# Attention products in tiles of 64 rows by 32 columns, with two accumulators for the weighing, on one Trainium2 core

## The chip, the cores and the metric

The kernel runs on one core of one Trainium2 chip. A core has TensorE (PE in the profile, with its weight loads as PEld), VectorE (DVE), ScalarE (ACT), GpSimd (POOL) and SyncE (SP, which here only issues DMAs). The metric is the device time of one execution in microseconds (us); the kernel before takes 2609.37 us, the median of three runs.

## The reference

One transformer block on 2048 tokens of width 576: attention of 32 heads (18 wide each), then a gated feed-forward part 4608 wide.

```python
qkv = (x @ wqkv).reshape(B, S, 3, H, Dh).transpose(2, 0, 3, 1, 4)
scores = jnp.einsum("bhqd,bhkd->bhqk", q, k) * Dh ** -0.5
p = softmax(scores);  o = jnp.einsum("bhqk,bhkd->bhqd", p, v)
h = x + A(layernorm(x))          # A: the attention above, then @ wo
out = h + B(layernorm(h))        # B: (gelu(z @ w_gate) * (z @ w_up)) @ w_down
```

## The kernel before, in words

Matrices that need more than 16 bits are held as a high and a low half-precision part, and a product is made of three matmuls or of stacked rows. A head is 18 wide; its Q and K are stacked as high and low parts in 54 rows (plus 2 rows that carry the row's maximum), and two heads share a tile, one from row 0 and one from row 64 (`half`).

The attention runs in 32 blocks n = 0 to 31: eight groups g of four heads, and for each group four query blocks qc of 512 queries. A block has 16 key tiles kt of 128 keys, and a key tile is one *step*. The string `STEPS[kt % 2]` sets the order of the work in a step by letters:

- `s`: `score` (L659 to L667). One matmul of 128 keys by 512 queries for one head, and ACT's exponential of it into SBUF (L667). Four in a step.
- `m`: `max_bank` (L607 to L625). The maxima for the *next* block: one matmul of 128 queries by 512 keys (L615), then a reduction over the keys. Of eight such units DVE alone reduces six (L625); for one pair ACT takes a Relu of a difference (L619, "over") and DVE finishes the pair with a fused add and maximum (L623, "both"). Four in a step.
- `w`: half a `weigh` (L669 to L677). Four matmuls (one for each head, 128 keys by 32 columns of V, in fp32) add the weighted values of the step before to an accumulator, for 256 of the 512 queries. V has a column of ones, so the accumulator also holds the softmax's divisor.
- `f`: two pieces of other matmul work (`fill`) and one piece of work for POOL (`side`).

Scores and maxima take turns in a ring of seven PSUM banks (`m_ring`), and the weighing's accumulator is the eighth (`singles[3]`, bank in the profile). At the end of a block `out_block` (L682) copies the accumulator to SBUF (L688, on DVE; for the last two blocks on ACT), fetches the divisors by DMA, takes reciprocals on POOL (L698 and on; on DVE in the last group), sends them back as rows by DMA, multiplies and splits on POOL (L711, L712, L713), and sends the result to the tensor XT (X in the profile) by DMAs on SP (L726 to L730). It is a generator: its parts are taken at key tiles 3 and 5 of the next block, in the last blocks (29 to 31) at 3 and 6.

In the last group two more things run beside the attention. `fill` is `wo_block` (from key tile 12 of blocks 29 to 31): the output projection of the query block that was just finished, as runs of 14 matmuls (L300) which read X; an `f` takes two runs. `side` is `split_early` on POOL (L1039 and on): it scales and splits the feed-forward weights (L1055, L1056, L1058, L1059) and then issues the next weights' DMAs on POOL's queue (L977, L979). The order of instructions on each engine is the order in which the program issues them.

## Time and profile before

| | |
|---|---|
| runs | 2608.49, 2609.37, 2609.64 us |
| profiled execution, span from first to last instruction | 2604.1 us, 53642 instructions |
| PE | 2579.3 us busy, 99% |
| DVE | 2010.0 us, 77% |
| ACT | 1661.3 us, 64% |
| POOL | 818.9 us, 31% |
| granted TensorE clock | 1.000 |
| plain attention block (1 to 28) | 35.84 us |
| blocks 29, 30, 31 | about 47.9, 49.1, 38.0 us |

The page gives no time of the profiled execution other than its span; the runs' median is 5.3 us longer. In a row of a timeline the columns are start, duration, engine, line, operation, output and inputs, shapes, count, and in brackets the idle time before it with what ended it. `nat`, `A`, `W`, `WK` and `X` are SBUF tensors of which parts are used for many things; `bank` and `quad` are PSUM banks.

### The profile page before, as it was taken

The numbers are of one execution on the slowest core, as the hardware profiler recorded it, in microseconds if no ns is written. First come the engines' busy times: TensorE is split into PE (matmuls) and PEld (weight loads), VectorE is DVE, ScalarE is ACT, GpSimd is POOL, SyncE is SP. The second block draws the span as 40 slices with busy tenths as digits, with TensorE's granted clock in tenths as the row PEclk, the third lists the DMA queues.
The fourth block names the chain that finished last, engine by engine and source line by source line (L and its number), as shares of the span: only waits on it lengthen the run. The fifth ranks groups of instructions, "written<-read, shape, count | busy, mean of one in ns | idle before, by whom it ended". The sixth has DMA issues, their size and how long they took to land.

```text
span 2604.1 us, 53642 instructions
## 1 busy us (share of the span) xinstructions
PE 2579.3 (99%) x20765; PEld 1198.2 (46%) x20765; DVE 2010.0 (77%) x3886; ACT 1661.3 (64%) x3124; POOL 818.9 (31%) x1146
## 2 busy tenths in 40 slices
PE   8999999999999999999999999999999999999999
PEld 4543333333333333333335555555555555555555
DVE  8479999999999999999867675757565656565653
ACT  6229999999999999999774543424243433333332
POOL 4302532322223232324585432323232323222221
PEclk9999999999999999999999999999999999999999
DMA  8621010101001010101135410101010101010110
GB/s 227 154 77 45 17 47 17 44 19 39 20 23 41 16 43 16 47 16 32 38 64 116 83 34 30 34 30 34 30 34 30 34 30 34 30 34 30 34 56 37
DMA packets 170193, 118.23 MB, mean 45 GB/s; under 512 B 88664, under 2 KB 147564, under 8 KB 169938
## 3 DMA queue, kind: packets, MB, share of 16 engines
q1 hardware_dynamic: 161198, 98.47, 14.2%
q0 software_dynamic: 8608, 16.33, 2.6%
q8 instruction: 162, 2.65, 0.4%
q14 instruction: 93, 0.76, 0.1%
q10 hardware_dynamic: 132, 0.01, 0.0%
HBM read 80.05 MB, written 15.01 MB: 37 GB/s over the span
## 4 chain that ended last, share of the span: by engine, by line
PE 92%; DVE 4%; POOL 1%; DMA 1%; issue 1%; ACT 1%; SPq 0%; POOLq 0%; ACTq 0%
PE bank L673 19%; PE bank L1125 15%; PE more L1125 15%; PE bank L300 11%; PE more L300 8%; PE quad L615 7%; PE bank L615 6%; PE quad L300 4%; PE quad L665 4%; DVE mx L625 3%; PE bank L665 3%; DVE nat L688 1%; DMA A<-qk_hi 0%; POOL A L1055 0%; ACT A L155 0%
## 5 line engine op out<-in xcount | busy, mean ns | idle before, releaser
L667 ACT ACTIVATE WK<-quad 128x512 f32<-128x512 f32 x1170 | 656.2, 621 | 23.4 <-PE quad L665 21.0
L673 PE MATMUL bank<-WK,V 128*32 128x256 f32 x8192 | 606.6, 388 | 2.7 <-DVE nat L688 0.6
L625 DVE TENSOR_REDUCE mx<-quad 128x1 f32<-128x512 f32 x836 | 553.8, 684 | 9.0 <-PE quad L665 1.5
L667 ACT ACTIVATE WK<-bank 128x512 f32<-128x512 f32 x878 | 504.9, 622 | 11.1 <-PE bank L665 9.3
L625 DVE TENSOR_REDUCE mx<-bank 128x1 f32<-128x512 f32 x716 | 477.1, 684 | 33.5 <-PE bank L615 26.4
L300 PEld LDWEIGHTS <-WK 128*128 128x128 f16 x3456 | 338.2, 98 | 88.3
L1125 PEld LDWEIGHTS <-W 128*128 128x128 f16 x2394 | 234.3, 98 | 278.3
L673 PEld LDWEIGHTS bank<-WK,V 128*32 128x32 f32 x8192 | 190.0, 108 | 268.2 <-issue 201.3
L300 PE MATMUL more<-W,WK 128*128 128x288 f16 x1728 | 235.2, 286 | 0.0
L300 PE MATMUL bank<-W,WK 128*128 128x288 f16 x1728 | 235.2, 286 | 0.0
L698 POOL TENSOR_TENSOR rp<-rc,minus_one 128x4 f32<-128x4 f32 x112 | 111.2, 1012 | 383.9 <-DMA rc<-nat 383.9
L1125 PE MATMUL bank<-X,W 128*128 128x512 f16 x792 | 223.8, 379 | 0.0
L1125 PE MATMUL bank<-V,W 128*128 128x512 f16 x720 | 202.4, 379 | 0.0
L993 POOL TENSOR_TENSOR A<-A 128x384 f32<-128x384 f32 x136 | 138.1, 1036 | 200.2 <-DMA A<-in_B_w_up_dram 83.7
L615 PE MATMUL quad<-W 54*128 54x512 f16 x514 | 191.0, 382 | 0.2 <-DVE mx L625 0.2
L615 PEld LDWEIGHTS <-W 54*128 54x128 f16 x1024 | 74.5, 94 | 241.3 <-issue 226.8
L1139 POOL TENSOR_TENSOR WK<-tmp,WK 128x512 f16<-128x512 f32 x73 | 88.5, 1212 | 305.8 <-ACT WK L1136 305.6
L615 PEld LDWEIGHTS <-A 54*128 54x128 f16 x1024 | 71.1, 94 | 231.0 <-issue 216.7
L1143 ACT COPY tmp<-more 128x512 f32<-128x512 f32 x36 | 20.9, 582 | 238.3 <-PE more L1125 203.4
L665 PE MATMUL quad<-A 56*128 56x512 f16 x584 | 172.1, 380 | 0.3
L615 PE MATMUL quad<-A 54*128 54x512 f16 x462 | 171.6, 382 | 0.1
L665 PE MATMUL quad<-W 56*128 56x512 f16 x586 | 167.5, 380 | 0.1
(348 smaller groups left out, 4122.3 us busy)
## 6 DMA issues: line engine op xcount, KB each, us to landing
A<-in_B_w_down_dram SPq DMA_DIRECT2D x8, 1152.0 KB
nat<-rc SPq DMA_DIRECT2D x32, 256.0 KB
A<-in_B_w_gate_dram SPq DMA_DIRECT2D x64, 128.0 KB
A<-in_B_w_up_dram SPq DMA_DIRECT2D x64, 128.0 KB
qk_hi<-tmp SPq DMA_DIRECT2D x36, 128.0 KB
qk_lo<-tmp SPq DMA_DIRECT2D x36, 128.0 KB
out_dram<-nat SPq DMA_DIRECT2D x16, 288.0 KB
X<-nat SPq DMA_DIRECT2D x100, 36.0 KB
```

The lines of the kernel that those rows point to most:

```text
L300: nc.tensor.matmul(dst, a, b, start=(i == 0), stop=(i == len(pairs) - 1))
L615: nc.tensor.matmul(pm[:, :TB], Q[r, q0 : q0 + P], keys, start=True, stop=True)
L625: nc.vector.tensor_reduce(dst, pm[:, :TB], axis=AX.X, op=ALU.max)
L665: nc.tensor.matmul(pS[:, :TB], K[r, kt * P : (kt + 1) * P], Q[r, qc * TB : (qc + 1) * TB], start=True, stop=True)
L667: nc.scalar.activation(pes[(2 * kt + hh // 2) % NPE][:, hh % 2], pS[:, :TB], AF.Exp, scale=ex_reg)
L673: nc.tensor.matmul(acc[32 * hh : 32 * hh + 32, qs], Vg[n // NB][:, kt * G4 + hh * VC : kt * G4 + hh * VC + 32], pes[(2 * kt + hh // 2) % N ...
L688: (nc.scalar.copy if n >= NS - 2 else nc.vector.tensor_copy)(oT, acc[:, :TB])
L698: nc.gpsimd.tensor_tensor(rc[:, c : c + 4], den[:, c : c + 4], minus_one.to_broadcast([P, 4]), op=ALU.pow)
L993: op(W8[:, d], W8[:, a], W8[:, b])
L1125: nc.tensor.matmul(bank, w, x_, start=start and i == 0, stop=i == len(mm) - 1, skip_group_check=not start)
L1139: nc.gpsimd.tensor_sub(hl[:, 2 * i + j], v, hh[:, 2 * i + j])
L1143: nc.scalar.copy(xg, g[0])
```

## The change

Every matmul of the attention is issued in tiles of 64 rows by 32 columns. A score or a maximum becomes four loads and four matmuls (L618, L670), each for 32 of its 128 output rows, on the row half of its head. Half a weighing becomes eight matmuls (L679): four columns by two row halves, and the two halves of the keys go to two accumulators, `singles[3]` and `quads[3]`. The ring has six banks instead of seven. `out_block` copies the first accumulator on ACT (L693) and the second on DVE, into `oT2`, and POOL adds the two (L696); for the last two blocks DVE adds the second one from PSUM. The steps have a new order, in which the halves of the weighing wait in a queue (one is taken in an even step, three in an odd one) and `f` comes last. The parts of `out_block` are taken one key tile later. The maxima come in an order in which two neighbours of one row half follow two of the other. Before the first block 93 maxima are taken ahead, 96 before.

```diff
--- before.py
+++ after.py
@@ -1,5 +1,6 @@
 import math
 from contextlib import ExitStack
+from collections import deque
 from itertools import chain, islice
 
 import concourse.bass as bass
@@ -573,6 +574,7 @@
     steps = [view(nat1, 12288 + 4 * TB * i, (HB, TB), F16) for i in range(2)]
     rows_of = ring([view(nat1, 18432 + 4 * TB * i, (TB,)) for i in range(2)])
     LOWEST = -3.0e38
+    CT = 32
     excess = []
     DQ = 4
     DI = TB // DQ
@@ -612,7 +614,9 @@
         r = half(h % 2, R1)
         pm = next(m_ring)
         keys = steps[g % 2][r, kc // 2] if kind == "over" else K[r, kc * TB : (kc + 1) * TB]
-        nc.tensor.matmul(pm[:, :TB], Q[r, q0 : q0 + P], keys, start=True, stop=True)
+        for c in range(0, P, CT):
+            nc.tensor.matmul(pm[c : c + CT, :TB], Q[r, q0 + c : q0 + c + CT], keys,
+                             start=True, stop=True)
         dst = mx[:, t, h, kc : kc + 1]
         if kind == "over":
             row = next(rows_of)
@@ -662,30 +666,36 @@
         pS = next(m_ring)
         Q, K = sets[g % 2][hh // 2]
         r = half(hh % 2, R1 + 2)
-        nc.tensor.matmul(pS[:, :TB], K[r, kt * P : (kt + 1) * P],
-                         Q[r, qc * TB : (qc + 1) * TB], start=True, stop=True)
+        for c in range(0, P, CT):
+            nc.tensor.matmul(pS[c : c + CT, :TB], K[r, kt * P + c : kt * P + c + CT],
+                             Q[r, qc * TB : (qc + 1) * TB], start=True, stop=True)
         nc.scalar.activation(pes[(2 * kt + hh // 2) % NPE][:, hh % 2], pS[:, :TB], AF.Exp, scale=ex_reg)
 
-    def weigh(n, kt, acc):
-        for q in range(2):
-            qs = slice(q * TB // 2, (q + 1) * TB // 2)
+    def weigh(n, kt, accs, q):
+        qs = slice(q * TB // 2, (q + 1) * TB // 2)
+        for i, acc in enumerate(accs):
+            ks = slice(64 * i, 64 * i + 64)
             for hh in range(4):
-                nc.tensor.matmul(acc[32 * hh : 32 * hh + 32, qs],
-                                 Vg[n // NB][:, kt * G4 + hh * VC : kt * G4 + hh * VC + 32],
-                                 pes[(2 * kt + hh // 2) % NPE][:, hh % 2, qs],
+                nc.tensor.matmul(acc[CT * hh : CT * hh + CT, qs],
+                                 Vg[n // NB][ks, kt * G4 + hh * VC : kt * G4 + hh * VC + CT],
+                                 pes[(2 * kt + hh // 2) % NPE][ks, hh % 2, qs],
                                  start=(kt == 0 and q == 0), stop=(kt == NT - 1 and q == 1))
-            yield
 
     minus_one = const.tile([P, 1], F32, name="minus_one")
     nc.gpsimd.memset(minus_one, -1.0)
 
-    def out_block(n, acc):
-
-
+    oT2 = view(nat1, 16384, (TB,))
+
+    def out_block(n, accs):
 
         g, qc = divmod(n, NB)
         oT = oTs[n % 2]
-        (nc.scalar.copy if n >= NS - 2 else nc.vector.tensor_copy)(oT, acc[:, :TB])
+        nc.scalar.copy(oT, accs[0][:, :TB])
+        if n < NS - 2:
+            nc.vector.tensor_copy(oT2, accs[1][:, :TB])
+            nc.gpsimd.tensor_add(oT, oT, oT2)
+        else:
+            nc.vector.tensor_add(oT, accs[1][:, :TB], oT)
         R = 4 * TB // P
         rc = small.tile([P, R], F32, tag="rc", name="rc")
         (nc.scalar if n == NS - 1 else nc.sync).dma_start(rc, oT.rearrange("(h c) q -> h c q", c=32)[:, DH].rearrange(
@@ -744,8 +754,8 @@
                 nc.gpsimd.memset(mx[:, :, 0, 1::2], LOWEST)
             for u in range(0, UPS, 2):
                 t, k = divmod(u, NB)
-                for unit in (("one", t, k, 1), (over, t, k + 1, 0), ("one", t, k + 1, 1), ("one", t, k, 2),
-                             ("one", t, k, 3), (both, t, k, 0), ("one", t, k + 1, 2), ("one", t, k + 1, 3)):
+                for unit in (("one", t, k, 1), ("one", t, k + 1, 1), ("one", t, k, 2), (over, t, k + 1, 0),
+                             ("one", t, k, 3), ("one", t, k + 1, 3), (both, t, k, 0), ("one", t, k + 1, 2)):
                     max_bank(n, mx, *unit)
                     yield
             max_finish(n, mx)
@@ -1246,40 +1256,40 @@
     side = iter(())
     take(fill, 18)
     for i in range(5 * AHEAD // 4):
-        take(mxs, 3 + (i % 5 == 4))
+        take(mxs, 1 if i == 5 * AHEAD // 4 - 1 else 3 + (i % 5 == 4))
         if i == AHEAD // 4:
             raw_loads()
         if i >= AHEAD // 3:
             take(sums)
         take(fill, 2 + (i % 5 == 2))
     run(sums)
-    m_ring = ring(singles[:3] + quads)
-    STEPS = ("ssmsmmfwmsw", "mssmssmfwwm")
-    OUT_AT = STEPS[0].rindex("w")
-    prev = None
+    m_ring = ring(singles[:3] + quads[:3])
+    accs = (singles[3], quads[3])
+    STEPS = ("smsmwsmsf", "wsmssmmwsmmwf")
+    halves = deque([None, None])
     for n in range(NS):
         g, qc = divmod(n, NB)
-        acc = singles[3]
         late = n > NS - NB
         for kt in range(NT):
             heads = iter(range(4))
-            halves = weigh(*prev) if prev is not None else iter(())
-            for step_no, step in enumerate(STEPS[kt % 2]):
+            for step in STEPS[kt % 2]:
                 if step == "s":
                     score(n, kt, next(heads))
                 elif step == "m":
                     take(mxs)
                 elif step == "w":
-                    take(halves)
-                    if kt == 0 and step_no == OUT_AT and prev is not None:
-                        ob = out_block(prev[0], prev[2])
-                        next(ob)
+                    half_ = halves.popleft()
+                    if half_ is not None:
+                        weigh(*half_)
+                        if half_[1] == NT - 1 and half_[3] == 1:
+                            ob = out_block(half_[0], accs)
+                            next(ob)
                 else:
                     if n < NS - 1 or kt < 11:
                         take(fill, 2)
                     take(side)
-            prev = (n, kt, acc)
-            if n and kt in ((1 if n == NS - 1 else 3, 6) if late else (3, 5)):
+            halves += [(n, kt, accs, q) for q in range(2)]
+            if n and kt in ((2 if n == NS - 1 else 4, 7) if late else (4, 6)):
                 take(ob)
             if late and kt == 11:
                 run(fill)
@@ -1308,8 +1318,9 @@
                              pause(2), until_ready(second))
     in_order.enter_context(tc.manual_schedule(engines={EngineType.SP}))
     run(side)
-    run(weigh(*prev))
-    ob = out_block(prev[0], prev[2])
+    for half_ in halves:
+        weigh(*half_)
+    ob = out_block(NS - 1, accs)
     next(ob)
     for _ in fill:
         take(rows, 2)
```

What stands on PE's queue in the middle of a block, before: a maximum, half a weighing, a maximum, a score, the other half (`quad` and `bank` are ring banks, bank_69 is the accumulator, A, W and WK hold Q, K and the exponentials).

```order
L615 MATMUL quad_76<-A 128x512
L673 MATMUL bank_69<-WK,V 32x256 x4
L615 LDWEIGHTS A
L615 MATMUL bank_66<-A 128x512
L665 LDWEIGHTS A
L665 MATMUL bank_67<-A 128x512
L673 MATMUL bank_69<-WK,V 32x256 x4
```

And now, at a like place, a maximum, a score and half a weighing; each of the first two stands there four times, once for each 32 of its output rows.

```order
L618 LDWEIGHTS W
L618 MATMUL quad_73<-W 32x512
...
L670 LDWEIGHTS A
L670 MATMUL quad_74<-A 32x512
...
L679 MATMUL bank_69<-WK,V 32x256 x4
L679 MATMUL quad_76<-WK,V 32x256 x4
```

The output of one matmul is 32 rows instead of 128, and the weighing has a second accumulator, quad_76, which was a bank of the ring.

ACT's queue at the start of a block, now: the copy of the first accumulator (bank_69) between exponentials. Before, no copy stood there except in the last two blocks.

```order
L672 ACTIVATE WK<-bank_66 128x512
L672 ACTIVATE WK<-bank_68 128x512
L693 COPY nat<-bank_69 128x512
L672 ACTIVATE WK<-quad_73 128x512
L672 ACTIVATE WK<-quad_75 128x512
```

POOL's queue in block 30, before: the end of a piece of weight splitting, the three instructions that make the rows of X, then the first two of eight weight DMAs (an L1055 and L1056 of the next piece come behind the eighth).

```order
L1058 TENSOR_TENSOR WK<-A,W 128x256
L1059 TENSOR_TENSOR W<-A,W 32x128
L711 TENSOR_TENSOR nat<-nat 128x512
L712 CAST nat<-nat 128x512
L713 TENSOR_TENSOR nat<-nat 128x512
L977 DMA A<-in_B_w_gate_dram 128x2x128
L979 DMA A<-in_B_w_gate_dram 96x1x128
```

And now the place from the eighth DMA on:

```order
L989 DMA A<-in_B_w_gate_dram 96x1x128
L1065 TENSOR_SCALAR A<-A,p_s_m_30894 128x768
L1066 CAST W<-A 128x768
L721 TENSOR_TENSOR nat<-nat 128x512
L722 CAST nat<-nat 128x512
L723 TENSOR_TENSOR nat<-nat 128x512
L1068 TENSOR_TENSOR WK<-A,W 128x512
```

The eight DMAs and the first two instructions of the next piece have passed ahead of the three that make X (L711 to L713 are L721 to L723 now). In block 29 the eight DMAs stood ahead already; there the new addition L696 stands at the head of the splitting, and one L1065 and L1066 more stand ahead of L721.

## The prediction, as put on record before the changed kernel ran

> **What bounds the kernel now.** I read the span first, then busy time by stretch, then the queues of each engine inside one stretch.

> ```profile
> core 0: 2604.1 us, clock 1.000
> ```

> ```profile
> 563.30:599.14 35.84, 35.76 (x390) 11.54 (x388) 35.31 (x67) 35.72 (x74) 8.39 (x14) 1.00 0.05 15
> 1244.50:1292.40 47.90, 44.97 (x449) 18.50 (x446) 40.68 (x85) 36.26 (x74) 32.42 (x45) 1.00 0.15 39
> 1292.40:1341.50 49.10, 48.00 (x473) 21.36 (x471) 27.21 (x59) 34.77 (x70) 34.66 (x57) 1.00 0.18 50
> ```

> The second fence is the view of busy time by stretch: after start, end and length come PE, PEld, DVE, ACT and POOL, each with its count, then the clock. The first row is one plain attention block of 35.84 us (16 key tiles), of which there are 28, blocks 1 to 28. Here PE, ACT and DVE all look full, so shares don't decide. The other two rows are blocks 29 and 30, which also carry the output projection of an earlier block; they are 12 and 13 us longer, and only PE is near full. So there are two stages with two limits. In the plain stage the question is which engine is full by its own rate. Groups of instructions over ten plain blocks, and ACT's and DVE's queues inside one:

> ```profile
> L667 ACT ACTIVATE WK<-quad 128x512 f32<-128x512 f32 x367 | 206.2, 622 | 0.6
> L667 ACT ACTIVATE WK<-bank 128x512 f32<-128x512 f32 x274 | 157.9, 621 | 0.5
> ```

> ```profile
> 703.62 0.65 ACT L667 ACTIVATE WK<-bank 128x512 f32<-128x512 f32 x1
> 704.10 0.67 ACT L619 ACTIVATE nat<-bank 128x512 f32<-128x512 f32 x1
> 704.58 0.68 ACT L667 ACTIVATE WK<-quad 128x512 f32<-128x512 f32 x1
> ```

> ```profile
> 703.82 1.28 DVE L625 TENSOR_REDUCE mx<-quad 128x1 f32<-128x512 f32 x2
> ```

> ACT ends at 704.27, 704.77 and 705.26: 0.49 us each, though a record is 0.65 long, since neighbours overlap. By the code ACT has 64 exponentials and 8 Relus in a block: 72 × 0.49 = 35.3 of 35.84, and the idle column is 1.1 us in ten blocks. ACT is full. A pair of DVE reductions takes 1.28, one alone 0.68, so one costs 0.60; 48 reductions, 8 double ones (L623) and one copy (L688) are 57 × 0.60 = 34.2 us, 1.6 below the block. Now PE over one step and the loads beside it:

> ```profile
> 701.19 1.07 PE L673 MATMUL bank<-WK,V 128*32 128x256 f32 x16
> 702.19 0.39 PE L615 MATMUL quad<-W 54*128 54x512 f16 x1
> 702.20 0.60 PE L665 MATMUL quad<-W 56*128 56x512 f16 x2
> 702.42 0.38 PE L665 MATMUL bank<-W 56*128 56x512 f16 x1
> 702.64 0.38 PE L615 MATMUL bank<-W 54*128 54x512 f16 x1
> 702.86 0.37 PE L615 MATMUL bank<-nat,W 54*128 54x512 f16 x1
> 702.86 0.39 PE L615 MATMUL quad<-W 54*128 54x512 f16 x1
> 703.18 0.64 PE L673 MATMUL bank<-WK,V 128*32 128x256 f32 x8
> 703.75 0.39 PE L615 MATMUL quad<-W 54*128 54x512 f16 x1
> ```

> ```profile
> 700.22 0.11 PEld L665 LDWEIGHTS <-W 56*128 56x128 f16 x2
> 700.23 0.10 PEld L615 LDWEIGHTS <-W 54*128 54x128 f16 x1
> ...
> 703.18 0.16 PEld L673 LDWEIGHTS bank<-WK,V 128*32 128x32 f32 x8 [0.23 <-issue]
> ```

> Score and maximum matmuls start 0.22 apart, two at a time where they sit on different row halves (702.86 twice). Sixteen weighing matmuls last 1.07 and eight 0.64, so eight cost 0.43, two slots of 0.22. The first weighing after a score starts 0.32 behind the last score (0.10 over a slot), and eight weighings last 0.57 until the next score (0.14 over two slots): a change between the two tile shapes costs about 0.12. Two steps (4.42 us) hold 16 scores and maxima in pairs, 8 slots, four half weighings, 8 slots, and six changes: 16 × 0.22 + 6 × 0.12 = 4.24. PE is close behind ACT, but ACT, not PE, sets the 35.84.

> **The change part by part.** *Tiles, plain stage.* A score is now four column tiles side by side on one row half, still one slot; a half weighing is eight tiles side by side, four columns by two halves, still 2 × 0.22. The six changes go: PE falls from 4.24 to 16 × 0.22 = 3.5 us per two steps. As ACT needs 9 × 0.49 = 4.41, this buys at most ACT's remaining idle time, 35.84 − 35.3 = 0.54 per block.

> *The second accumulator.* DVE keeps its copy (now of the second accumulator), POOL gets an addition, and ACT gets the copy of the first, in the queue of the full engine: 0.49 per block. With PE's slack taking all of the old idle time, a block is 73 × 0.49 = 35.75 (−0.09); with all of it staying, 36.33 (+0.49). The idle time sat mostly around DVE's copy and the end of a block's maxima, where PE now has 0.9 us per two steps to catch up, but six banks in the ring instead of seven hold less work for ACT (6 × 0.49/2 on average, since about half go to DVE). I take −0.02 per block, near the low end: 28 × −0.02 = **−0.5**, bounds −2.5 and +14.

> *Records.* Two steps issue 256 loads and matmuls instead of 96, so 17 ns for each in 4.42 us. The densest row above is eight loads within 0.16 us, each about 0.10 long: (0.16 − 0.10)/7 = 9 ns apart. The longest possible reading is 32 records in the 1.00 us of the sixteen weighings, 31 ns, but that stretch is explained by four slots of array time. I take 9 ns, so nothing; the other end is a rival below.

> *Loads.* A score's load of 0.10 is now four loads on 32 columns each. At 700.22 to 700.23 three loads of both halves run together while the matmuls of both halves are just beginning, so a load waits for no slot, and the sum has nothing for it. [...]

> *Late blocks, tiles.* Ten times in blocks 29 to 31 a step carries 28 full-size projection matmuls:

> ```profile
> 1285.51 3.59 PE L300 MATMUL quad<-W,X 128*128 128x288 f16 x28
> ```

> Those steps are PE's: a step of 8 slots is 1.76, and 3.59 comes on top, against 2.2 of ACT. Of about three shape changes in such a step two go, since the projection still uses the whole array: 2 × 0.12 = 0.24, times ten: **−2.4**, bounds −1 and −5 (all changes of the steps around it too).

> *Late blocks, POOL.* The projection needs the X rows of the block before, which out_block makes on POOL (L711, L712 and L713; L721 to L723 now) and SP sends. PE already waits for them:

> ```profile
> 1273.43 1.64 PE L300 MATMUL quad<-W,X 128*128 128x288 f16 x12
> 1276.85 0.41 PE L300 MATMUL quad<-W,X 128*128 128x288 f16 x2 [1.77 <-POOL A L1044]
> ```

> ```profile
> 1324.80 1.64 PE L300 MATMUL quad<-W,X 128*128 128x288 f16 x12
> 1327.15 0.40 PE L300 MATMUL quad<-W,X 128*128 128x288 f16 x2 [0.71 <-DMA X<-nat]
> ```

> The first wait is put down to a POOL instruction done long before; the rows show that it is the same wait, 1.77 and 0.71 us. So what delays POOL here delays the end. POOL's rows, with DVE's copy:

> ```profile
> 1247.26 2.21 POOL L1055 TENSOR_SCALAR A<-A,p_s_m 128x768 f32<-128x768 f32 x1 [13.74 <-DVE pi_gsc L171]
> ...
> 1266.55 1.28 POOL L711 TENSOR_TENSOR nat<-nat 128x512 f32<-128x512 f32 x1
> ...
> 1315.26 1.28 POOL L711 TENSOR_TENSOR nat<-nat 128x512 f32<-128x512 f32 x1 [1.13 <-DMA nat<-rc]
> ...
> 1318.40 0.84 POOL L977 DMA_DIRECT2D A<-in_B_w_gate_dram  x1
> ...
> 1324.29 2.23 POOL L1055 TENSOR_SCALAR A<-A,p_s_m 128x768 f32<-128x768 f32 x1
> 1326.59 0.82 POOL L1056 CAST W<-A 128x768 f16<-128x768 f32 x1
> ```

> ```profile
> 1248.10 0.68 DVE L688 COPY nat<-bank 128x512 f32<-128x512 f32 x1
> ```

> In block 29 the new addition (priced like L711, 1.28) stands ahead of the weight-splitting chain, which began at 1247.26, ahead of the copy's end at 1248.78. It now begins at 1248.78 + 1.28 = 1250.1, 2.9 later, and POOL has no gap from there to 1266.55. Since out_block's last part is taken one key tile later, one more pair L1065 and L1066 (2.23 + 0.82) stands ahead of L721: 2.9 + 3.05 = 5.9 late. The projection's slot is now the last of its step, behind about 1 us of weighing and scores, so 5 us of it are new waiting. In block 30 the eight weight DMAs (1318.40 to 1324.29, 5.9) and one more pair (3.05) pass ahead of L721, which POOL could have begun at 1314.13, 1.13 before the divisor's DMA released it: 5.9 + 3.05 − 1.13 = 7.8, less 1 = 7. SP's sends and everything on PE behind the projection shift with it; there is no cover, as ACT's queue drains meanwhile. **+12** together; bounds 0 (the whole slide lies under a slower PE) and 15.

> Sum: −0.5 − 2.4 + 12 = **+9**. On the profiled 2604.1 that is 2613; the median of the runs, 2609.37, is 5.3 above the profiled span (start and end that the trace leaves out), which stays: about **2619 us**.

> **The rivals.**

> *No stall, tiles alone.* Key tile 12 of the late blocks may come later relative to POOL than I count, or POOL's chain may be released later than the addition anyway (the 13.74 us idle at 1247.26 speaks for room, the 1.77 and 0.71 against). Then −0.5 − 2.4 remains: about 2606, no change that counts.

> *Faster.* The same, with the steady idle time all gone (−2.5) and the large PE gain of the late steps (−5): 2609.4 − 7.5 = 2602. For it speaks that PE is at 99.8% in the plain block; against it that ACT has 0.54 us of room and receives 0.49.

> *The ring starves ACT.* Six banks instead of seven; the copy for which the next weighing waits sits behind ACT's queued exponentials. From the point where a block keeps its old idle time and adds the copy, it costs 0.49 × 28 = +14 beside the late stall: 2619 + 14 = 2633. Against it: PE is 0.9 us ahead per two steps.

> *PE becomes the bound.* If each slot's load were exposed, 16 × 0.10 = 1.6 us come on 3.5: 5.1 per two steps against 4.48. The same results from 20 ns a record (256 × 20); the point from which it decides is 17 ns. Over 28 × 8 pairs of steps that is 0.64 × 224 = +143: 2753. Nine ns between loads speak against it. [...]

> **How the numbers follow.** The forecast has 0.50 and its own range 2610 to 2628; no stall 0.20; faster 0.13; the starved ring 0.10; PE as the bound 0.07. A run of this kernel can tell about 0.2%, 5.2 us, from no change, so "same" is 2604.2 to 2614.6. Faster is the third case and the lucky end of the second: 0.15. Same is most of the second and the low end of the forecast: 0.28. The rest, 0.57, is slower. For 8 in 10 the range leaves out PE as the bound and the far ends of two other cases: **2602 to 2636**.

> **What would show it.** Steady blocks of 35.7 to 35.9 with ACT's waits near nothing and PE's share well below full show the plain stage right; 36.3 shows the ring. In blocks 29 and 30, waits of about 7 and 8 us at the projection's last matmuls, released by X, show the stall; waits under 2 us make the forecast wrong. A load or matmul cadence over 17 ns with ACT waiting for scores all along would show PE as the bound.

## The result: 2.7% slower

| | before | changed kernel |
|---|---|---|
| median | 2609.12 us | 2679.68 us |
| span of the profiled execution | 2604.1 us | 2678.4 us |
| mean granted TensorE clock | 1.000 | 0.985 |

The ratio is 1.0273, 95% interval 1.0258 to 1.0287: 70 us slower, where 2619 (2602 to 2636) was forecast. All runs list their span 1.8 us below their time, so, if the profiled execution of before is like them, the 5.3 us that the prediction put outside the span were 1.8, and 3.5 by which that one execution was quicker than its median.

Where the time went is seen best from the starts of the exponentials, 64 to a block. By them the two spans split like this (us; "seven pairs" are blocks 1, 4, 8, 12, 16, 20 and 24, each with the block behind it):

| | before | changed | difference |
|---|---|---|---|
| to the first exponential | 204.9 | 206.0 | +1.1 |
| block 0 | 35.6 | 35.1 | -0.5 |
| seven pairs, 14 blocks | 501.8 | 560.3 | **+58.6** |
| the other 14 blocks of 1 to 28 | 502.7 | 501.8 | -0.9 |
| blocks 29 to 31 | 134.5 | 151.5 | **+16.9** |
| behind the last exponential | 1224.6 | 1223.8 | -0.8 |

The view of busy time by stretch of the changed kernel (start and end, length, PE, PEld, DVE, ACT, POOL, clock, DMA), for block 8, the block behind it, the plain block 15, and blocks 29 and 30:

```profile
508.61:552.09 43.48, 36.04 (x1030) 20.40 (x1022) 35.23 (x68) 36.21 (x74) 18.71 (x32) 0.95 0.22 55
552.09:589.62 37.53, 37.45 (x1033) 21.79 (x1041) 35.38 (x66) 36.07 (x74) 9.68 (x15) 0.92 0.07 18
776.47:812.24 35.77, 35.61 (x1033) 20.78 (x1033) 35.08 (x67) 35.77 (x75) 9.68 (x15) 1.00 0.09 23
1303.12:1361.48 58.36, 51.18 (x1138) 30.69 (x1138) 42.17 (x90) 36.68 (x74) 34.93 (x48) 0.91 0.14 35
1361.48:1417.84 56.36, 49.58 (x1036) 29.49 (x1028) 27.59 (x62) 34.75 (x69) 37.17 (x61) 0.91 0.17 45
```

The plain block is what the prediction said: 35.77 us, ACT busy for all of it. (PE's busy column is 35.61 there, so the prediction's sign that PE would be well below full did not come.) But block 8 has the same work in 43.48, with PE, DVE and ACT each idle for 7 to 8 us, and in the block behind it PE has hardly any idle time and a clock of 0.92. PE's queue at that place names the wait:

```profile
543.85 0.40 PE L679 MATMUL quad<-WK,V 64*32 64x256 f32 x4
551.36 0.61 PE L670 MATMUL bank<-A 56*32 56x512 f16 x4 [7.11 <-DMA A<-mT]
```

The first score of block 9 waits 7.11 us for the maxima of its rows, which `max_finish` sends from mT into Q. Behind the wait a score's four matmuls last 0.61, where 0.40 is what they took ahead of it (540.64), and the clock column says why:

```profile
543.90:552.10 8.20, 1.00 (x28) 0.15 (x16) 0.74 (x3) 0.95 (x3) 0.00 (x0) 0.72 0.11 26
552.10:556.00 3.90, 3.90 (x76) 1.99 (x76) 2.57 (x5) 2.89 (x6) 0.00 (x0) 0.50 0.08 15
556.00:560.00 4.00, 4.00 (x116) 2.83 (x112) 3.80 (x9) 3.59 (x8) 1.66 (x2) 0.77 0.07 15
```

PE stood still from 544.25, was given half its clock (0.50) from 547.6, and had it until 557.8. With this goes the 1.8 us by which block 9 is longer than the plain block. In blocks 0 to 28 the waits for mT are seven, 6.2 to 8.3 us each and 47.0 in all (in each row below: the sum, how many, the longest); the other 11.6 of the pairs' 58.6 us lie behind them, where the clock is low.

```profile
PE quad L670 <- DMA A<-mT: 14.9, 2, 8.3
PE bank L670 <- DMA A<-mT: 13.3, 2, 7.1
PE bank L670 <- DMA W<-mT: 12.4, 2, 6.2
PE quad L670 <- DMA W<-mT: 6.4, 1, 6.4
```

Why does mT come late? SP's queue in block 8, of the changed kernel and then of before (block start 508.61 and 492.05):

```profile
534.69 3.92 SPq L736 DMA_DIRECT2D X<-nat  x5
538.71 6.51 SPq L604 DMA_DIRECT2D kd<-nat  x8
545.40 0.71 SPq L606 DMA_DIRECT2D nat<-kd  x2
546.15 1.15 SPq L645 DMA_TRANSPOSE mT<-mm  x1
...
549.57 2.75 SPq L651 DMA_DIRECT2D A<-mT  x4
```

```profile
514.34 3.93 SPq L726 DMA_DIRECT2D X<-nat  x5
518.37 1.92 SPq L641 DMA_TRANSPOSE mT<-mm  x1
520.34 3.31 SPq L602 DMA_DIRECT2D kd<-nat  x4
523.77 2.76 SPq L647 DMA_DIRECT2D A<-mT  x4
```

Two things differ. The eight sends of `key_steps` (kd, 6.5 us, the next group's key differences) stand ahead of mT's transposition, not behind it. And X, which stands ahead of both, goes 26.1 us into the block instead of 22.3. The first follows from the number of maxima taken ahead: with 93 instead of 96, and three and five maxima in a step instead of four and four, the finishing comes with the first maximum of key tile 9, and `key_steps` is issued behind key tile 8. (SP's queue in this stage is put in order by a planner, as four kd sends between mT's transposition and its sends show in before; in the changed kernel it kept the kd sends ahead. The sentence ahead of the prediction that each engine follows the program's order does not hold for SP.) The second shows on POOL, in the changed kernel and before:

```profile
511.46 1.28 POOL L696 TENSOR_TENSOR nat<-nat 128x512 f32<-128x512 f32 x1 [16.96 <-ACT nat L693]
512.69 0.63 POOL L569 DMA_DIRECT2D W<-qk_hi  x1
...
519.98 3.98 POOL L708 TENSOR_TENSOR rp<-rc,minus_one 128x4 f32<-128x4 f32 x4
```

```profile
490.72 0.63 POOL L568 DMA_DIRECT2D W<-qk_hi  x1 [13.98 <-PE bank L615]
...
498.90 3.99 POOL L698 TENSOR_TENSOR rp<-rc,minus_one 128x4 f32<-128x4 f32 x4 [1.21 <-DMA rc<-nat]
```

Twelve DMAs of the next group's Q and K stacks are issued by POOL in this block. Before, they began 1.3 us ahead of the block. Now the addition L696 stands at their head and waits for the accumulators' copies, so they begin 4.1 us into it, and the reciprocals behind them (L698, now L708) begin at 11.4 instead of 6.9.

In blocks 29 and 30 the waits that the prediction named are there:

```profile
1336.04 0.90 PE L301 MATMUL quad<-W,X 128*128 128x288 f16 x3 [3.28 <-DMA X<-nat]
1340.51 0.64 PE L301 MATMUL quad<-W,X 128*128 128x288 f16 x2 [3.56 <-DMA X<-nat]
...
1394.01 0.87 PE L301 MATMUL quad<-W,X 128*128 128x288 f16 x3 [2.07 <-DMA X<-nat]
1398.71 0.64 PE L301 MATMUL quad<-W,X 128*128 128x288 f16 x2 [3.83 <-DMA X<-nat]
```

6.84 and 5.90 us, where 1.77 and 0.71 were before.

### The profile page after: what moved, and what is told of

Read it like the earlier page. It is cut to its first block, busy times and chain, and to the rows that moved or that the text cites. A ratio compares the mean times of both kernels' runs of the same rounds, so it can differ in the third digit from the quotient of the medians.

```text
span 2678.4 us, 96899 instructions
## 1 busy us (share of the span) xinstructions
PE 2591.2 (97%) x41245; PEld 1495.0 (56%) x41245; DVE 2003.9 (75%) x3888; ACT 1666.6 (62%) x3154; POOL 856.7 (32%) x1176
## 3 DMA queue, kind: packets, MB, share of 16 engines
q1 hardware_dynamic: 161198, 98.47, 13.7%
## 4 chain that ended last, share of the span: by engine, by line
PE 78%; POOL 6%; DMA 4%; DVE 4%; issue 3%; SPq 3%; ACT 1%; POOLq 0%; DVEq 0%; ACTq 0%
PE bank L1135 14%; PE more L1135 14%; PE bank L301 10%; PE more L301 8%; PE quad L679 6%; PE bank L679 5%; PE quad L618 5%; PE bank L618 5%; PE quad L301 4%; PE bank L670 4%; PE quad L670 3%; DVE mx L629 2%; SPq L604 1%; POOL rp L708 1%; DMA A<-qk_hi 1%
## 5 line engine op out<-in xcount | busy, mean ns | idle before, releaser
L672 ACT ACTIVATE WK<-bank 128x512 f32<-128x512 f32 x1109 | 726.3, 750 | 70.7 <-PE bank L618 27.5
L679 PE MATMUL bank<-WK,V 64*32 64x256 f32 x8192 | 660.1, 385 | 2.2 <-ACT nat L693 0.3
L679 PE MATMUL quad<-WK,V 64*32 64x256 f32 x8192 | 647.0, 384 | 1.9 <-DVE nat L698 1.7
L679 PEld LDWEIGHTS bank<-WK,V 64*32 64x32 f32 x8192 | 238.6, 107 | 35.6 <-ACT WK L672 12.4
L679 PEld LDWEIGHTS quad<-WK,V 64*32 64x32 f32 x8192 | 226.7, 106 | 18.1 <-DVE nat L698 2.2
L670 PEld LDWEIGHTS <-A 56*32 56x32 f16 x4096 | 149.0, 92 | 145.6 <-issue 58.9
L670 PE MATMUL bank<-A 56*32 56x512 f16 x2220 | 207.6, 386 | 14.2 <-DMA A<-mT 13.3
L670 PE MATMUL bank<-W 56*32 56x512 f16 x2216 | 207.0, 389 | 12.9 <-DMA W<-mT 12.4
L670 PEld LDWEIGHTS <-W 56*32 56x32 f16 x4096 | 146.3, 92 | 128.5 <-issue 53.5
L1003 POOL TENSOR_TENSOR A<-A 128x384 f32<-128x384 f32 x136 | 137.7, 1033 | 201.5 <-ACT tmp L1140 82.8
L618 PE MATMUL quad<-W 54*32 54x512 f16 x2040 | 199.0, 386 | 1.5 <-DVE mx L629 0.6
L618 PEld LDWEIGHTS <-W 54*32 54x32 f16 x4096 | 132.5, 90 | 110.7 <-issue 96.9
L670 PE MATMUL quad<-A 56*32 56x512 f16 x1876 | 173.9, 384 | 16.1 <-DMA A<-mT 14.9
```

The lines of the kernel that those rows point to most:

```text
L618: nc.tensor.matmul(pm[c : c + CT, :TB], Q[r, q0 + c : q0 + c + CT], keys, start=True, stop=True)
L670: nc.tensor.matmul(pS[c : c + CT, :TB], K[r, kt * P + c : kt * P + c + CT], Q[r, qc * TB : (qc + 1) * TB], start=True, stop=True)
L672: nc.scalar.activation(pes[(2 * kt + hh // 2) % NPE][:, hh % 2], pS[:, :TB], AF.Exp, scale=ex_reg)
L679: nc.tensor.matmul(acc[CT * hh : CT * hh + CT, qs], Vg[n // NB][ks, kt * G4 + hh * VC : kt * G4 + hh * VC + CT], pes[(2 * kt + hh // 2) % ...
L1003: op(W8[:, d], W8[:, a], W8[:, b])
```

## The experiments

Theory A: the order of `key_steps` and the finishing of the maxima. Rivals: B, out_block's parts taken one key tile later; C, the small tiles bring the clock down; D, the number taken ahead as such; later E, the addition on POOL. The table gives each run by the stages above, as in its own trace; each is beside 2607 to 2609 us for before on its chip. Not listed are block 0 (35 to 36 us; 38 to 39 in ahead96, before_ks7 and ahead101_wide, 42.6 in before92) and what lies behind the last exponential (1224 to 1225 in all).

| run | median, us | ratio (interval) | to first exp. | seven pairs | other 14 | blocks 29-31 |
|---|---|---|---|---|---|---|
| before | 2609.1 | | 204.9 | 501.8 | 502.7 | 134.5 |
| changed | 2679.7 | 1.0273 (1.0258-1.0287) | 206.0 | 560.3 | 501.8 | 151.5 |
| ks9 | 2644.8 | 1.0131 (1.0115-1.0148) | 205.3 | 520.1 | 508.2 | 152.6 |
| ahead96 | 2706.0 | 1.0368 (1.0351-1.0385) | 206.9 | 541.1 | 542.0 | 152.4 |
| before92 | 2805.9 | 1.0752 (1.0734-1.0770) | 204.2 | 596.6 | 596.6 | 139.9 |
| ks9_ob36 | 2635.2 | 1.0095 (1.0078-1.0112) | 207.1 | 517.9 | 507.4 | 140.6 |
| ahead101 | 2649.0 | 1.0146 (1.0129-1.0163) | 212.0 | 519.6 | 503.5 | 153.8 |
| before_ks7 | 2656.6 | 1.0184 (1.0167-1.0201) | 204.0 | 549.4 | 503.4 | 136.0 |
| ahead101_dve | 2624.1 | 1.0056 (1.0039-1.0073) | 215.3 | 506.3 | 505.8 | 134.1 |
| ahead101_wide | 2721.4 | 1.0428 (1.0410-1.0445) | 211.8 | 546.3 | 540.8 | 162.6 |
| ks5 | 2657.5 | 1.0184 (1.0167-1.0201) | 205.2 | 537.2 | 501.6 | 151.3 |
| ks5_late | 2643.8 | 1.0131 (1.0114-1.0148) | 206.0 | 539.4 | 501.6 | 135.6 |
| ob35 | 2676.1 | 1.0253 (1.0236-1.0270) | 207.8 | 557.0 | 501.5 | 149.9 |
| dve7_ks9 | 2633.9 | 1.0100 (1.0083-1.0117) | 205.1 | 512.9 | 501.9 | 151.9 |
| dve7_ks9_late | 2620.4 | 1.0044 (1.0027-1.0061) | 211.1 | 511.6 | 502.0 | 136.7 |

**ks9: the finishing ahead of key_steps.**

```diff
-            if g + 1 < NG and kt == 8 and qc == (1 if g == 0 and NB > 1 else 0):
+            if g + 1 < NG and kt == 9 and qc == (1 if g == 0 and NB > 1 else 0):
                 key_steps(g + 1)
```

> The changed kernel with one number changed: the key differences of the next group (key_steps) are issued behind key tile 9 instead of 8, so behind the finishing of the maxima (max_finish, L638 to L651) on POOL's and SP's queues and not ahead of it. Theory A, queue order: the seven waits of 7 to 9 us at the first score of a block, with the slow clock behind them, come from this order alone (blocks 1, 4, 8, 12, 16, 20, 24 and the ones behind them are together 59 us over 35.77 each). It expects 2679.7 - 59 = 2621 us, no wait for a DMA of mT over 1 us, and a mean clock above 0.99. Rival B, the later out_block: its X sends (3.9 us on SP) one key tile later are what holds SP, so half of the wait stays: 2650 us or more. Rival C, the throttle: 256 small tiles in two steps bring the clock down by themselves; then the clock stays at 0.985 and the time above 2670.

2644.8. The pairs lose 40 of the 58.6 us and the clock rises to 0.992 with the same tiles, so the order is a cause and rival C is out. But 18 stay, and smaller waits for mT (up to 3.1 us, 15.6 in all) appear one block later, so that the blocks outside the pairs are 6 us longer: `key_steps` now ends so late that the next block's divisors (rc) wait behind it on SP, and leave 11.5 us into block 5 instead of 7.7. Net, the 28 blocks lose 34. A alone does not close the sum.

**ahead96 and before92: the finishing moved by the number taken ahead.**

```diff
-        take(mxs, 1 if i == 5 * AHEAD // 4 - 1 else 3 + (i % 5 == 4))
+        take(mxs, 3 + (i % 5 == 4))
```

```diff
-        take(mxs, 3 + (i % 5 == 4))
+        take(mxs, 0 if i == 5 * AHEAD // 4 - 1 else 3 + (i % 5 == 4))
```

> The changed kernel with 96 maxima taken ahead of the first block, as before, instead of 93; key_steps stays behind key tile 8. The finishing of the maxima comes with the 33rd maximum of a block, in key tile 8, ahead of key_steps. Theory A (queue order) expects the same as with key_steps moved, 2621 us within 5. Rival B (the later out_block) and rival C (the throttle by small tiles) expect no change, 2680 us.

> The kernel before with 92 maxima taken ahead instead of 96, and nothing else: the finishing of the maxima then comes with the first maximum of key tile 9, behind key_steps on POOL and SP, in the old tiles and the old order. Theory A (queue order) expects the waits here too, seven times 7 to 9 us and the slow clock behind them: 2609 + 59 = 2668 us. Rivals B and C, which need the later out_block or the small tiles, expect 2609 us.

Both moved something else. With 96 the waits at the seven blocks are gone (the pairs are as long as the other blocks), but every block takes 38.6; with 92 in the kernel before every block takes 42.61. One block of before92, in which PE is the fullest engine, and one of ahead96, in which PE and ACT both have 1.5 us or more to spare:

```profile
545.07:587.68 42.61, 41.21 (x385) 12.38 (x384) 36.17 (x67) 36.98 (x74) 15.66 (x28) 1.00 0.23 55
```

```profile
515.90:554.50 38.60, 36.51 (x1033) 19.62 (x1025) 35.02 (x67) 37.05 (x74) 18.73 (x32) 1.00 0.22 60
```

The number sets where the maxima's order of eight stands against the order of a step, and with it which scores and maxima meet a partner on the other row half. In a block of before, 16 of the 128 start with no other within 0.1 us, in one of before92 48; the 16 more slots of 0.22 that this makes are, as an estimate, 3.5 of the 6.8 us. The rest, and how it goes in ahead96, no run takes apart. As tests of A the two runs are confounded.

**ahead101: a whole turn of eight more.**

```diff
-        take(mxs, 1 if i == 5 * AHEAD // 4 - 1 else 3 + (i % 5 == 4))
+        take(mxs, 9 if i == 5 * AHEAD // 4 - 1 else 3 + (i % 5 == 4))
```

> The changed kernel with 101 maxima taken ahead instead of 93: eight more, a whole turn of the maxima's order, so that scores and maxima pair as with 93 on the two row halves; key_steps stays behind key tile 8. The finishing of the maxima then comes with the first maximum of key tile 7, ahead of key_steps. Theory A (queue order): the seven waits go and the pairing stays, so blocks of 35.8 us throughout and 2679.7 - 59 = 2621 us, up to 5 less or more for what key_steps still delays in the block behind. Rival D (what 96 ahead showed, longer steps, comes from the number taken ahead as such, not from the pairing): blocks of 38 us or more, 2690 or more.

Plain blocks are 35.82, so rival D is out: what counts is where in its turn the order of eight stands, not the number. The pairs lose 40.8, as with ks9, and 18 stay again; taking eight more costs 6 us at the start.

**before_ks7: A in the kernel before.**

```diff
-            if g + 1 < NG and kt == 8 and qc == (1 if g == 0 and NB > 1 else 0):
+            if g + 1 < NG and kt == 7 and qc == (1 if g == 0 and NB > 1 else 0):
                 key_steps(g + 1)
```

> The kernel before with key_steps behind key tile 7 instead of 8, and nothing else: old tiles, old order of a step, 96 ahead. The eight kd sends (6.5 us) and two loads then stand ahead of the mT transposition on SP, as in the changed kernel. The finishing comes in key tile 8 here, one key tile earlier than in the changed kernel, so theory A (queue order) expects a wait of about 3 us at the first score of seven blocks and some slow clock behind it: 7 x 3.5 = +25, 2634 us. Rivals B (the later out_block) and C (the small tiles) expect 2609.

2656.6: the pairs lengthen by 47.6 us in old tiles and old order, twice what was expected. The waits for mT sum to 24.7 us (the longest, ahead of block 17, is below); the rest lies behind them, where eight weighings take 1.08 us instead of 0.64. A is shown as sufficient, without any part of the change.

```profile
846.86 0.60 PE L665 MATMUL quad<-A 56*128 56x512 f16 x1 [6.10 <-DMA A<-mT]
```

**ks5: the sends in SP's free time.**

```diff
-            if g + 1 < NG and kt == 8 and qc == (1 if g == 0 and NB > 1 else 0):
+            if g + 1 < NG and kt == 5 and qc == (1 if g == 0 and NB > 1 else 0):
                 key_steps(g + 1)
```

> The changed kernel with key_steps behind key tile 5 instead of 8, 93 ahead, nothing else. The eight kd sends then go out while SP has nothing to do (between 18.3 and 26.1 us of block 8 in the changed kernel) and stand neither ahead of mT in this block, as behind key tile 8, nor ahead of the next block's divisors, as behind key tile 9. Theory A+B (the wait is the kd sends ahead of mT, about 7 us, on top of a chain of out_block that is 3.8 us later than before, where before had 1.3 us to spare): mT's rows land at 35 of 35.8 us, so no wait over 1 us anywhere in blocks 1 to 28, 59 us less: 2620 us within 4, clock above 0.99 (what is left is in blocks 29 and 30). If something else holds the blocks, 2640 or more as behind key tile 9.

2657.5, a miss: the pairs lose 23 only. The sends did go out early, but two of them went ahead of the divisors' rows (nat<-rc), which leave SP 20.4 us into block 8 instead of 17.7, and X comes later with them:

```profile
532.85 3.10 SPq L736 DMA_DIRECT2D X<-nat  x4
535.99 1.65 SPq L591 DMA_DIRECT2D nat<-qk_hi  x2
537.75 1.16 SPq L645 DMA_TRANSPOSE mT<-mm  x1
538.95 2.34 SPq L591 DMA_DIRECT2D nat<-qk_lo  x3
541.40 2.73 SPq L651 DMA_DIRECT2D A<-mT  x4
```

Most of X goes 30 us into block 8 (which starts at 502.93), later than in the changed kernel (26.1), and the planner puts five more loads (L591) around mT.

**ob35: out_block's parts earlier (rival B).**

```diff
-            if n and kt in ((2 if n == NS - 1 else 4, 7) if late else (4, 6)):
+            if n and kt in ((2 if n == NS - 1 else 4, 7) if late else (3, 5)):
```

> The changed kernel with the parts of out_block taken at key tiles 3 and 5 again in blocks 1 to 28 (late blocks as changed); key_steps stays behind key tile 8 and 93 are taken ahead, so the kd sends stay ahead of mT. Theory A+B: X and what follows on SP come one key tile, 2.2 us, earlier, so each of the seven waits falls by about that and its slow clock by 0.3: -18, 2662 us. If the queue order were all of it: 2680. If the later out_block were all of it (rival B alone): 2621.

The pairs lose 3.3 us of the 18 expected: B is out, and with it my reading of ks9's rest. X did not move (26.3 us into block 8). That POOL's queue is held by L696 and the twelve DMAs, whatever comes behind them, would explain this, and made theory E.

**ahead101_dve: no addition on POOL** (with the edit of ahead101).

```diff
-        nc.scalar.copy(oT, accs[0][:, :TB])
-        if n < NS - 2:
-            nc.vector.tensor_copy(oT2, accs[1][:, :TB])
-            nc.gpsimd.tensor_add(oT, oT, oT2)
-        else:
-            nc.vector.tensor_add(oT, accs[1][:, :TB], oT)
+        (nc.scalar.copy if n >= NS - 2 else nc.vector.tensor_copy)(oT, accs[0][:, :TB])
+        nc.vector.tensor_add(oT, accs[1][:, :TB], oT)
...
-            if n and kt in ((2 if n == NS - 1 else 4, 7) if late else (4, 6)):
+            if n and kt in ((1 if n == NS - 1 else 3, 6) if late else (4, 6)):
```

> 101 ahead, the parts of out_block in the late blocks at key tiles 3 and 6 (1 and 6) as before, and both accumulators read by DVE (a copy and an addition from PSUM) instead of ACT's copy, DVE's copy and POOL's addition; blocks 30 and 31 keep ACT's copy. ACT is back at 72 operations in a block, DVE goes to 58. Theory (ACT sets the plain block): 72 x 0.49 = 35.3 and what idle time is left, 0 to 0.2, so 0.3 to 0.5 less in each of 28 blocks, -8 to -14; the late stage loses 9.5 (measured with key tiles 3 and 6) and up to 3 more for the addition: 2621 - 11 - 11 = 2599 us. Rival (DVE is next, 58 x 0.60 + the finishing's 0.22 = 35.0 and its waits): blocks of 35.8 as with 101 ahead, 2610 us.

2624.1. The pairs are 506.3, as long as the other blocks, and blocks 29 to 31 are back at 134.1. But a plain block is 36.05, not 35.4: DVE's two reads stand one behind the other, and once in a block ACT runs dry behind them (0.56 us named here; the starts are 1.35 us apart, where 0.48 is usual):

```profile
434.80 0.69 DVE L694 TENSOR_TENSOR nat<-quad,nat 128x512 f32<-128x512 f32 x1
...
435.54 0.64 PE L679 MATMUL quad<-WK,V 64*32 64x256 f32 x8 [0.16 <-DVE nat L694]
...
436.50 0.60 ACT L672 ACTIVATE WK<-bank 128x512 f32<-128x512 f32 x1 [0.56 <-PE bank L670]
```

**dve7_ks9: both causes taken away.**

```diff
-        if n < NS - 2:
+        if n not in (0, 3, 7, 11, 15, 19, 23) and n < NS - 2:
             nc.vector.tensor_copy(oT2, accs[1][:, :TB])
...
-            if g + 1 < NG and kt == 8 and qc == (1 if g == 0 and NB > 1 else 0):
+            if g + 1 < NG and kt == 9 and qc == (1 if g == 0 and NB > 1 else 0):
```

> The changed kernel with two edits: key_steps behind key tile 9 (so behind the finishing of the maxima), and in the seven blocks whose out_block meets the next group's stack loads (n = 0, 3, 7, 11, 15, 19, 23) DVE adds the second accumulator from PSUM, so that no L696 stands on POOL ahead of the twelve stack DMAs that POOL issues. Theory A+E (the waits have two causes, each sufficient for a part: the kd sends ahead of mT on SP, and L696 holding POOL until the accumulators are copied, by which the twelve DMAs start at 4.1 us of the block instead of before its start, L708 at 11.4 instead of 6.9, and X, mT 3.8 us later): no wait of PE for mT over 1 us, all plain blocks 35.8 to 36.4 and 2622 us within 5. If L696 is not the reason for what was left behind key tile 9 and with 101 ahead, the waits of 1 to 4 us stay: 2645.

The pairs are 512.9 and the other blocks 501.9: the 28 blocks lose 47, 13.5 more than by the order alone. POOL's DMAs begin 1.9 us ahead of the block again, and one wait for mT over 1 us is left (2.3 us more in block 21). Of the 11 us that stay in the pairs, 2.9 are DVE's addition (0.41 in seven blocks, 36.18 for 35.77), and 6 are stalls of another kind in blocks 4 and 24 (last section). The median, 2633.9, is 12 above the 2622 expected, in good part for these. Theory A+E holds for the waits, with that one exception. The addition was taken away only together with the order, so what it costs by itself in the changed kernel is not shown.

**ks9_ob36 and dve7_ks9_late: the late blocks.** The first is ks9 with `(1 if n == NS - 1 else 3, 6) if late`; the second is dve7_ks9 with that and with DVE's addition in blocks 28 and 29.

> The changed kernel with key_steps behind key tile 9, and with the parts of out_block in blocks 29 to 31 taken at key tiles 3 and 6 (1 and 6 in block 31) as before. L721 then stands ahead of the eight weight DMAs in block 30 and ahead of one pair L1065 and L1066 in block 29, but the addition L696 stays. Theory A for the late stage (POOL's order holds X): the waits of 6.84 and 5.90 us at the projection's last matmuls fall to about 3.7 and 0 (+2.9 for the addition stays in block 29), and half of the slow-clock time of some 4 us goes: 12 us below the kernel with key_steps moved alone, about 2609 us. Rival: the late stage is longer because of the new step order or the tiles; then 2621 us, as with key_steps moved alone.

> The same with the late blocks mended too: the parts of out_block at key tiles 3 and 6 (1 and 6) as before, and DVE's addition in blocks 28 and 29, which took 13.7 us beside key_steps at key tile 5. Theory: 2622 - 13.5 = 2609 us, 2604 to 2612, the same as the kernel before within what can be told: tiles and second accumulator by themselves neither cost nor bring anything in the plain blocks, since ACT sets them. If the tiles bring something of their own: under 2604.

Blocks 29 to 31 go from 152.6 to 140.6 by the order on POOL alone, 12.0 us as expected (the median fell by 9.5, as the start took 1.8 longer), and to 136.7 by the addition. The waits that were expected to fall from 6.84 and 5.90 to 3.7 and 0 fell to 4.14 and 0.99 by the order. The same pair beside ks5 took 13.7 off the median (2643.8; expected 2608, since ks5 had not done its part):

> key_steps behind key tile 5, the parts of out_block in the late blocks at key tiles 3 and 6 (1 and 6) as before, and in the late blocks (28 and 29) the second accumulator added by DVE from PSUM instead of DVE's copy and POOL's addition. The late stage loses 9.5 (measured with the order alone) and up to 3 for the addition that stood ahead of the splitting in block 29: 2620 - 12 = 2608 us, within the kernel before's 2609 +- 4, as the prediction's sum has it without its stall term: 2606. If the addition costs nothing: 2611.

The late stage is thus settled: POOL's order and addition are 15 to 16 us of it, and what is left lies 0 to 2 us from before. dve7_ks9_late as a whole is 2620.4, 11 above the 2609 expected; its start took 6 us longer in the profiled execution. No version here beats the kernel before.

**ahead101_wide: scores and maxima as wide tiles again** (with the edit of ahead101).

```diff
-        for c in range(0, P, CT):
-            nc.tensor.matmul(pS[c : c + CT, :TB], K[r, kt * P + c : kt * P + c + CT],
-                             Q[r, qc * TB : (qc + 1) * TB], start=True, stop=True)
+        nc.tensor.matmul(pS[:, :TB], K[r, kt * P : (kt + 1) * P],
+                         Q[r, qc * TB : (qc + 1) * TB], start=True, stop=True)
```

The same in `max_bank`.

> 101 ahead, with scores and maxima as single matmuls of 128 output rows again, the weighing in 64 by 32 tiles. Theory of the prediction (ACT sets the plain block, PE has slack): the tile changes come back, 0.12 each, five in two steps by the new order (w in three places, two of them within a step): PE at 3.5 + 0.7 = 4.2 of 4.41, so blocks within 0.3 us of the kernel with 101 ahead, and 2 to 4 us more in the late blocks: 2621 to 2632 us. Rival (one tile shape is what keeps the steps at ACT's pace, since PE waits in its order for banks): blocks over 37, above 2655 us.

2721.4, the rival's side: 38.56 for each block. PE's queue in it:

```profile
500.87 0.42 PE L676 MATMUL bank<-WK,V 64*32 64x256 f32 x4
...
501.46 0.39 PE L667 MATMUL bank<-W 56*128 56x512 f16 x1
501.46 0.39 PE L617 MATMUL bank<-A 54*128 54x512 f16 x1
501.69 0.38 PE L617 MATMUL quad<-A 54*128 54x512 f16 x1
501.69 0.38 PE L667 MATMUL bank<-W 56*128 56x512 f16 x1
502.00 0.42 PE L676 MATMUL bank<-WK,V 64*32 64x256 f32 x4
```

Half a weighing and two pairs take 1.13 us: four slots of 0.22 and 0.25 for two changes of tile shape, which is the 0.12 that the prediction read from before. The new order weighs in four places of two steps, so it has eight changes, where the old had six and the expectation five. With 4 × 1.13 = 4.5 and the slots of matmuls without a partner (502.60 to 503.13 has one), PE is behind ACT's 4.41. The new order of a step needs the one tile shape, and the one shape, the copy on ACT counted in, buys next to nothing in the plain blocks: 501.8 to 502.0 against 502.7.

## Why the prediction was wrong

- **What bounds the plain blocks: right.** 35.77 for 35.84 us; the prediction took -0.02 per block, 14 undisturbed blocks show -0.07. By the trace ACT's operations start 0.48 us apart where nothing holds them, not 0.49: 72 of them left 1.4 us of a block before, 73 leave 0.9 now. So the idle time fell by about 0.5, and the copy took 0.48 of that again, which is the balance that the prediction drew up.
- **PE's slack, records and loads: right in effect.** Blocks with 1033 matmuls and as many loads run at ACT's pace. 128 matmuls and their loads go in 4.47 us (an eighth of 35.77), 35 ns for each pair; PE as the bound (2753, for which loads and matmuls had to need 5.1 us) did not come. How much slack PE has is not shown: its busy column stays at 35.61 of 35.77.
- **The ring of six: right, no sign of it** in undisturbed blocks.
- **Late blocks, tiles, -2.4:** not seen. With POOL mended, blocks 29 to 31 take 134.1 (ahead101_dve) to 136.7, against 134.5.
- **Late blocks, POOL, +12: right in mechanism.** The stretches take 16.9 more in all. The waits are 6.84 and 5.90, +10.3 over before. The term was too small, since it had no price for the clock, which is 0.50 for 10.24 us in each of the two blocks (from 1336.1 and 1394.1; 0.91 over blocks 29 and 30).
- **The step that failed** is the sum of the plain stage, "28 × −0.02 = **−0.5**": one plain block stood for all 28, and in 14 of them, the seven pairs, the runs showed +58.6. Two terms were put at nothing there without a reason. In "The second accumulator", "POOL gets an addition" stands without a price in the plain blocks; and that 93 maxima are taken ahead was told with the change, and priced nowhere. I read POOL's and SP's queues only in blocks 29 and 30. In the seven blocks that load the next group, the same two views would have shown 1.3 us to spare between the end of mT's sends (34.5 us into block 8) and the block's end (35.84), the kd sends of 6.5 us next to it, and twelve stack DMAs behind the place of L696. An estimate from these rows would have been a slide of 3.8 for L696 and of 6.5 for the sends, less 1.3: 9 in each of seven blocks, +63, against waits of 47.0 and 11.6 behind them. By the runs, the order alone is 34 us of the 57.7 in the 28 blocks, the addition with it 13.5 more; with all additions on DVE and 101 ahead the pairs are no longer than the other blocks (506.3 and 505.8).

The prediction's test for being wrong, "waits under 2 us" in the late blocks, did not come; it was the place, not the size, that was missed.

## What to carry to other kernels

A count that only shifts a stage by a few items (93 for 96) also moves everything issued at the wrap of that count: list what stands next to it on the DMA-issuing queues, in the rare blocks as well as in the common ones. An instruction that waits for the end of a stage must not be put on a queue that issues the next stage's DMAs, however small it is (here 1.28 us, and the twelve DMAs behind it began 4.1 us into the block instead of 1.3 ahead of it): price it by what stands behind it. Where an engine is full with little to spare, a kernel's steps are tuned to one phase and one tile shape (a block took 42.61 us for 35.84 with 92 taken ahead, and 38.56 for 35.82 with wide tiles), and a test that changes either measures that and not the question.

## What the runs showed of the hardware

```profile
424.13:427.54 3.41, 1.69 (x48) 0.66 (x43) 2.03 (x4) 2.28 (x5) 0.00 (x0) 1.00 0.10 20
427.54:430.95 3.41, 2.81 (x56) 1.27 (x64) 1.39 (x3) 1.35 (x3) 0.00 (x0) 0.50 0.03 7
```

```profile
996.04:999.46 3.42, 2.13 (x60) 0.87 (x51) 2.50 (x5) 2.71 (x6) 0.00 (x0) 1.00 0.12 28
999.46:1002.87 3.41, 2.22 (x63) 0.91 (x69) 1.89 (x4) 1.79 (x3) 0.00 (x0) 1.00 0.03 7
1002.87:1006.28 3.41, 3.33 (x104) 1.91 (x96) 3.13 (x6) 3.39 (x8) 1.28 (x1) 1.00 0.00 0
```

From 230 to 1500 us, 69 cells at full clock had 1.70 us or more without a matmul; 68 of them were followed by a cell at 0.50, and of 51 cells with 0.8 to 1.7 us, 7 were. In the changed kernel it was nine of nine (1.80 to 3.41 us without a matmul). The one exception is the wait of 1.77 us in before (1276.85); the same wait in before_ks7 (1327.17) was followed by 0.50. So half a cell without a matmul (1.70 us) was enough in all cells but one; what else counts is not shown.

- **PE waited for no semaphore in the midst of heavy DMA.** With both causes taken away, block 24 of dve7_ks9 has this, while stack loads of the next group run (the DMA engines are busy 0.51 of the time from 1083 to 1085):

```profile
1084.77 0.62 PE L670 MATMUL quad<-A 56*32 56x512 f16 x4 [1.87 <-issue]
```

The packets of the instruction queue number 322 in the changed kernel and 162 before (16 KB each); two of them are 6.4 us apart just there, at 1075.62 and 1082.00, where eight came in 35 us (565 to 600) of the changed kernel, one in 4.4. That PE had run out of instructions is the author's guess from these numbers, and is not shown: no run took the loads or the instructions away.
